# Two slices of the first feed-forward block placed among the first attention, its out products in the bank of its scores, head pairs in turns in the score product

## The chip, the cores and the metric

The kernel runs on one core of a Trainium2 chip. A core has a matrix engine (TensorE, "PE" in the profile; its weight loads are listed apart as "PEld"), a vector engine (VectorE, "DVE"), a scalar engine (ScalarE, "ACT"), a general engine (GpSimd, "POOL") and a queue that issues the transfers (SyncE, "SP"). Each engine works through its own queue in order and they wait for each other by semaphores. The metric is the device time of one execution in microseconds (us); the time of a kernel is the median of several runs.

## The reference: what is computed

Causal attention with a memory term, then two gated feed-forward blocks, on 4 sequences of 576 tokens with 8 heads of 64 (a model width of 512), all in float32:

```python
scores = scale * q @ k^T            # masked causally, softmax over the keys
local  = softmax(scores) @ v
q_p    = where(q > 0, q, exp(q) - 1) + 1
mem    = (q_p @ M_prev) / (q_p @ z_prev + 1e-06)
x      = g * mem + (1 - g) * local  # g = sigmoid(beta), one per head
x      = x / sqrt(mean(x * x) + 1e-06) * rms_g
x      = (silu(x @ w_gate) * (x @ w_val)) @ w_out          # 512 -> 1536 -> 512
x      = (sigmoid(x @ w_gate2) * (x @ w_val2)) @ w_out2    # 512 -> 1536 -> 512
```

The weights arrive as float64 (`in_w8`), are read as 16-bit pieces and put together as float32 on the core.

## The kernel before

**Groups of tokens.** The work is cut into five groups `g`. Group -1 holds the first 128 tokens of all four sequences (512 columns), groups 0 to 3 hold the other 448 tokens of one sequence each. For every group the attention comes first and then the two feed-forward blocks `l = 0, 1`, each in 12 slices `f` of 128 hidden units (`NF`). `hidden` computes one slice: gate product `pg` and value product `pv` (`mm3`, 12 matmuls each, L511), tanh on ScalarE (L526) and two products on VectorE (L528, L529). `out_share` multiplies the slice with its part of `w_out` into four PSUM banks `po0` to `po3` (L545 for group -1, L548 for the others).

**The attention of the next group rides along.** While group `g` is in its feed-forward blocks, the attention of group `g + 1` is issued in 34 steps (`att_steps`), some after each `out_share`: `att_v` (loads v into `x`), then for each head `att_qk` (loads `kd`, `qd`; L164 to L169), `att_scores` (L182 to L302), `att_av`, and for each pair of heads `att_mem`, at the end `att_norm` and four `att_xT`. Only group -1 has nothing to ride on: its attention, `att_first`, stands at the head of the kernel.

**The first attention.** For each sequence b, `att_scores0` runs once for the even heads (j = 0) and once for the odd (j = 1): one matmul writes the mask over a whole bank `po{(2b+j) % 4}` (L210), four matmuls of 64 rows add the scores of four heads (L219), VectorE takes the maxima (L221, L222), ScalarE the exponentials (L226), TensorE transposes the four blocks in place (L231), ScalarE copies them to SBUF (L235). `att_mem` makes the memory term: `e = exp(q)` on ScalarE (L347), `min(e, 1)` and `max(q, 0)` on GpSimd (L349, L350), and two matmuls per pair of heads, one for `e` and one for `q` (L369); `mem_out` (L335 to L339) writes `x`. For the sequence before, `att_av0` makes the out products (L244) in a bank of the pool `psm` (two banks, tag `mm`, the same that `pg` and `pv` use), VectorE scales them (L316 to L320) and GpSimd adds them to `x` (L248). `att_norm` squares `x` on ScalarE (L391) and takes the root on GpSimd (L396), `att_xT` scales `x` into `xn` (L401), transposes it on TensorE (L406) and splits the result into a high part (ScalarE, L410) and a low part (VectorE, L411): that is `xt`, the input of the feed-forward.

**Weights.** `weights(g, l, f)` returns gate, value and output weights of a slice (m = 0, 1, 2). In group -1 each is loaded raw (512 KB, `load_raw`, L456), put together on ScalarE and VectorE (L462, L465), written back to DRAM for the later groups (`kept`, 256 KB, L496), and gate and value are split into two parts (L425, L426). The raw pieces use 4 buffers of the pool `wp` and 2 of the later pool `wl`; the split weights use a ring of `NEARLY = 3` buffers in `wp` and `NLATE = 4` in `wl`.

**Memory.** The tiles of the first attention lie in a pool `zp` that is closed when `att_first` has been traced. The pools `hp` (output weights `wo`, the slice tiles `t` and `h`) and `wl` are opened behind it and take the same memory, so each of their tiles waits until the tiles of `zp` under it have had their last use.

**Order.** A planner at build time gives each engine its queue: it takes the instructions in the order of the program as they become ready on its own estimate of the times, so a later instruction that is ready can stand ahead of an earlier one that isn't. `issue_after(i)` keeps the instructions of a block behind `i` in the queue of `i`'s engine. In the kernel before the weights and steps that are traced up to slice 3 stand behind the last maxima and exponentials of the first attention (L624, L625); from then on there is no such bound. The last part reads, in short:

```python
xt = att_first()
zctx.close()
early_ws = [weights(-1, 0, f) for f in range(2)]     # slices 0 and 1
for o, m in ((0, 256), (256, 256)):                  # first the columns of sequences 0 and 1
    for f in range(early):
        hidden(ws[f], l, f, m, g, xt, hs[f], o)
```

## Time and profile before

| what | us |
|---|---|
| runs, median (lowest to highest of 3) | 1108.96 (1106.51 to 1110.95) |
| the profiled execution, its own time | 1107.19 |
| the profiled execution, its span (first to last instruction) | 1105.4 |
| TensorE busy in the span | 1084.5 |
| VectorE busy | 684.2 |
| ScalarE busy | 484.5 |
| GpSimd busy | 86.1 |

The profile is of one execution. Its span is 1.8 us shorter than the time of the same execution, and that time is 1.8 us below the median of the runs. Busy times of the engines overlap. The mean granted TensorE clock over the span was 0.987 of full speed (full is 2.4 GHz, the lower level 1.2 GHz).

### The profile page before, as it was taken

Reading aid. Unit: us, or ns where it says so; the run is one execution under the profiler, and the core shown is the slowest. Engines: PE = TensorE matmul, PEld = TensorE weight load, DVE = VectorE, ACT = ScalarE, POOL = GpSimd, SP = SyncE. Lnnn points to the kernel's source line nnn. Section 1 sums busy time; section 2 is a strip of 40 time slices with the busy share of each in tenths; the row PEclk is TensorE's granted clock in tenths of the full one; section 3 lists DMA queues with packets and bytes.
Section 4 is the critical chain, followed back from the end, with each engine's and each line's share of the span. In section 5 each row is a group of like instructions: output and inputs, shape, how many; then the busy total and the mean of one; then the engine's idle time right before and its main releaser. Section 6 shows DMA issues by size and latency. Waiting matters only on the chain.

```text
span 1105.4 us, 17395 instructions
## 1 busy us (share of the span) xinstructions
PE 1084.5 (98%) x6420; PEld 940.3 (85%) x6420; DVE 684.2 (62%) x1373; ACT 484.5 (44%) x905; POOL 86.1 (8%) x70
## 2 busy tenths in 40 slices
PE   8889999999999999999999999999999999999997
PEld 6766676767779999999999899999989999999997
DVE  5796869766678899866666855656785542222111
ACT  6575557655456556544344533333354322112111
POOL 4300000100000010100100100000101000000000
PEclk8889999999999999999999999999999999999999
DMA  9398878876899988978866666786655557776650
GB/s 329 108 317 297 260 243 258 249 252 204 300 333 339 357 282 307 314 240 268 249 210 209 215 211 208 251 262 207 222 190 192 198 185 245 217 218 216 213 168 34
DMA packets 93844, 264.61 MB, mean 239 GB/s; under 512 B 11072, under 2 KB 17216, under 8 KB 93632
## 3 DMA queue, kind: packets, MB, share of 16 engines
q1 hardware_dynamic: 93760, 263.50, 72.3%
q8 instruction: 51, 0.84, 0.3%
q14 instruction: 33, 0.27, 0.1%
HBM read 202.12 MB, written 61.34 MB: 238 GB/s over the span
## 4 chain that ended last, share of the span: by engine, by line
PE 92%; DMA 3%; DVE 2%; ACT 1%; issue 1%; POOL 0%; SPq 0%; ACTq 0%; DVEq 0%
PE pg L511 27%; PE pv L511 27%; PE po L548 21%; PE po L545 7%; PE ps L182 4%; PE pm L369 1%; PE pav L308 1%; PE pav L310 1%; DMA raw<-in_w 1%; PE pav L309 1%; PE pxt L406 1%; DMA rawl<-in_w 1%; DMA ph<-in_qT 1%; DMA qk<-in_qk 0%; DMA kd<-in_kT 0%
## 5 line engine op out<-in xcount | busy, mean ns | idle before, releaser
L526 ACT ACTIVATE t<-pg 128x448 f32<-128x448 f32 (+2 forms) x122 | 66.4, 544 | 185.1 <-PE pg L511 184.9
L533 ACT CAST h<-t 128x448 fp32r<-128x448 f32 x96 | 54.2, 564 | 126.4 <-DVE t L531 68.7
L292 POOL PARTITION_ALL_REDUCE mb<-mx x32 | 57.2, 1789 | 629.0 <-DVE mx L288 532.1
L531 DVE SCALAR_TENSOR_TENSOR t<-t,pv 128x448 f32<-128x448 f32 (+1 forms) x60 | 37.8, 630 | 94.4 <-PE pv L511 90.5
L545 PE MATMUL po<-t,wo 128*128 128x512 f32 x192 | 86.6, 594 | 0.0
L534 DVE TENSOR_TENSOR h<-t,h 128x448 fp32r<-128x448 f32 x96 | 60.4, 629 | 33.2 <-ACT h L533 32.6
L548 PE MATMUL po<-h,wr 128*128 128x448 f32 x360 | 79.6, 365 | 0.0
L548 PE MATMUL po<-h,wl 128*128 128x448 f32 x348 | 77.3, 368 | 0.2 <-ACT h L533 0.2
L528 DVE SCALAR_TENSOR_TENSOR t<-t,pg 128x448 f32<-128x448 f32 (+2 forms) x62 | 38.1, 615 | 59.4 <-ACT t L526 59.0
L548 PEld LDWEIGHTS po<-h,wr 128*128 128x128 f32 x360 | 66.7, 188 | 4.5
L173 ACT ACTIVATE sc<-sc 128x1536 f32<-128x1536 f32 x32 | 47.6, 1488 | 51.6 <-DVE sc L301 42.5
L548 PEld LDWEIGHTS po<-h,wl 128*128 128x128 f32 x348 | 64.9, 188 | 6.0 <-ACT h L533 0.5
L264 ACT COPY sc<-ps 128x448 f32<-128x448 f32 (+3 forms) x128 | 47.4, 374 | 51.5 <-DVE sc L259 33.0
L545 PEld LDWEIGHTS po<-t,wo 128*128 128x128 f32 x192 | 36.4, 191 | 36.4 <-issue 34.4
L511 PE MATMUL pv<-xt,wl 128*128 128x448 f32 (+2 forms) x276 | 63.4, 374 | 3.0 <-DVE t L529 2.9
L511 PE MATMUL pg<-x,wl 128*128 128x448 f32 (+1 forms) x252 | 61.7, 384 | 0.3 <-ACT t L526 0.3
L511 PE MATMUL pv<-x,wl 128*128 128x448 f32 (+1 forms) x264 | 62.0, 377 | 0.0
L176 DVE TENSOR_TENSOR pt<-sc,pt 128x1536 f16<-128x1536 f32 x32 | 56.1, 1754 | 7.6 <-ACT pt L175 7.6
L511 PEld LDWEIGHTS pv<-xt,wl 128*128 128x128 f32 x276 | 51.0, 196 | 8.3 <-DVE t L529 3.1
L511 PE MATMUL pg<-xt,wl 128*128 128x448 f32 (+1 forms) x252 | 57.7, 375 | 0.0
L548 PE MATMUL po<-h,ws 128*128 128x448 f32 x264 | 57.0, 363 | 0.0
L182 PE MATMUL ps<-qq,kk 128*128 128x448 f32 (+2 forms) x160 | 55.0, 348 | 1.9 <-ACT sc L257 1.2
(154 smaller groups left out, 2448.0 us busy)
## 6 DMA issues: line engine op xcount, KB each, us to landing
wl<-parts SPq DMA_DIRECT2D x68, 512.0 KB, 3.7
wr<-parts SPq DMA_DIRECT2D x68, 512.0 KB, 4.0
ws<-parts SPq DMA_DIRECT2D x48, 512.0 KB, 3.9
raw<-in_w SPq DMA_DIRECT2D x48, 511.8 KB, 5.3
w<-kept SPq DMA_DIRECT2D x72, 256.0 KB, 4.9
wrl<-parts SPq DMA_DIRECT2D x32, 512.0 KB, 3.5
kept<-w SPq DMA_DIRECT2D x48, 256.0 KB, 3.9
rawl<-in_w SPq DMA_DIRECT2D x24, 511.8 KB, 5.3
```

The source lines that it names most:

```text
L173: nc.scalar.activation(out=sc[:, 0:n], in_=sc[:, 0:n], func=AF.Exp, scale=scale)
L176: nc.vector.tensor_tensor(out=pt[:, 1, 0:n], in0=sc[:, 0:n], in1=pt[:, 0, 0:n], op=ALU.subtract)
L182: nc.tensor.matmul(ps[:, c0:c0 + n], kk[:, k0:k0 + 128], r[:, q0:q0 + n], start=(i == 0), stop=(i == 1 and not mask))
L264: nc.scalar.copy(out=sc[:, d:d + n], in_=ps[:, c:c + n])
L292: nc.gpsimd.partition_all_reduce(mb[:, 0:448], mx[:, 0:448], channels=128, reduce_op=bass_isa.ReduceOp.max)
L511: nc.tensor.matmul(ps[:, 0:n], w[:, a, k * 128:(k + 1) * 128], x[:, b, k, o:o + n], start=(i == 0), stop=(i == 3 * KD - 1))
L526: nc.scalar.activation(out=t, in_=pg[:, 0:n], func=AF.Tanh, scale=0.5)
L528: nc.vector.scalar_tensor_tensor(out=t, in0=t, scalar=1.0, in1=pg[:, 0:n], op0=ALU.add, op1=ALU.mult)
L533: nc.scalar.copy(out=hh[:, 0, 0:n], in_=t)
L534: nc.vector.tensor_tensor(out=hh[:, 1, 0:n], in0=t, in1=hh[:, 0, 0:n].bitcast(F32), op=ALU.subtract)
L545: nc.tensor.matmul(po[d][:, 0:n], w[2][:, c], t[:, 0:n], start=(f == 0), stop=(f == NF - 1))
L548: nc.tensor.matmul(po[d][:, 0:n], w[2][:, a, c], hh[:, b, 0:n], start=(f == 0 and i == 0), stop=(f == NF - 1 and i == 2))
```

## The change

- Slices 0 and 1 are begun inside `att_first`: their gate and value weights are requested before the first scores, and the first half of each slice (the 256 columns of sequences 0 and 1) is traced behind the transposed input of sequence 1 (slice 0) and of sequence 2 (slice 1). The second halves (`hidden(..., 256)`) stay behind the first attention. For this the ring of split weights is 4 buffers in `wp` and 3 in `wl`, and the tile `t` moves to `wp`, so neither depends on `zp`. The output weights (m = 2) of the two slices are requested after the first attention, as before, and the pool `wl` is opened ahead of `hp`.
- The out products of the first attention go to the bank that held the scores of the same sequence and head parity, so `psm` is left to `pg` and `pv`.
- In the score product the two head parities take turns: q and k of the even heads are in rows 0 to 63, of the odd heads in rows 64 to 127, and the matmuls alternate between them, into two banks.
- In the memory term `max(q, 0)` moves from GpSimd to VectorE as one instruction that also adds it to `e`; there is one matmul per pair of heads where there were two. `e` has two buffers for four sequences, so `exp(q)` of sequences 2 and 3 waits until the square of sequence 0 or 1 has used `e` as its scratch. The scaled scores and `xn` use fewer or other buffers (`xn` takes the place of q).
- The copy of the transposed weights of the odd heads goes from ScalarE to VectorE.
- All steps of group 0's attention that are traced in group -1 stand behind the last instructions of the first attention on ScalarE and VectorE (L410 and L411 for sequence 3).

```diff
--- before.py
+++ after.py
@@ -26,8 +26,8 @@
 SO = (0, 448, 896, 1216, 1408)
 SW = 1536
-NEARLY = 3
-NLATE = 4
+NEARLY = 4
+NLATE = 3
 NRAW = 4
@@ -190,54 +190,60 @@
     def att_load0():
         for b in range(B):
-            z["e", b] = zp.tile([128, NMAX], F32, tag=f"ze{b}", name="e0")
+            z["e", b] = zp.tile([128, NMAX], F32, tag=f"ze{b % 2}", name="e0")
             qk = zp.tile([128, 2, NMAX], F32, tag=f"zqk{b}", name="qk0")
             z["q", b], z["k", b] = qk[:, 0], qk[:, 1]
             nc.sync.dma_start(out=qk, in_=qk0[b])
-            for j in range(2):
-                z["s", b, j] = zp.tile([128, NMAX], F32, tag=f"zs{b}{j}", name="s0")
             if b == 1:
                 z["v"] = zp.tile([128, B, NMAX], F32, tag="zv", name="v0")
                 nc.sync.dma_start(out=z["v"], in_=v[:, 0:128, :].rearrange("b s d -> s b d"))
             if b < 2:
                 first_raw.append(load_raw(0, 0, b))
-    def att_scores0(b, j):
-        q, k, sc = z["q", b], z["k", b], z["s", b, j]
-        r = slice(64 * j, 64 * j + 64)
-        ps = pso.tile([128, NMAX], F32, tag=f"po{(2 * b + j) % 4}", name="ps0")
-        nc.tensor.matmul(
-            ps.rearrange("p (a k) -> p a k", a=NP),
-            tri_b,
-            ident_b[:, None, :].to_broadcast([128, NP, 128]),
-            start=True,
-            stop=False,
-        )
+    def att_scores0(b):
+        q, k = z["q", b], z["k", b]
+        pss = [pso.tile([128, NMAX], F32, tag=f"po{(2 * b + j) % 4}", name="ps0") for j in range(2)]
+        for ps in pss:
+            nc.tensor.matmul(
+                ps.rearrange("p (a k) -> p a k", a=NP),
+                tri_b,
+                ident_b[:, None, :].to_broadcast([128, NP, 128]),
+                start=True,
+                stop=False,
+            )
         for p in range(NP):
             c = slice(128 * p, 128 * p + 128)
-            nc.tensor.matmul(ps[:, c], q[r, c], k[r, c], start=False, stop=(p == NP - 1))
-        m = ap_.tile([128, NP], F32, tag="m0", bufs=2, name="m0")
-        nc.vector.tensor_reduce(out=m, in_=ps.rearrange("p (a k) -> p a k", a=NP), op=ALU.max, axis=AX.X)
-        z["dve", b, j] = nc.vector.tensor_scalar(out=m, in0=m, scalar1=-scale, scalar2=None, op0=ALU.mult)
-        rs = ap_.tile([128, NP], F32, tag="rs", bufs=4, name="rs")
-        for p in range(NP):
-            c = slice(128 * p, 128 * p + 128)
-            z["act", b, j] = nc.scalar.activation(
-                out=sc[:, c], in_=ps[:, c], func=AF.Exp, scale=scale, bias=m[:, p:p + 1], accum_out=rs[:, p:p + 1]
-            )
-        for p in range(NP):
-            c = slice(128 * p, 128 * p + 128)
-            nc.tensor.transpose(ps[:, c], sc[:, c], ident)
-        if j == 0:
-            z["p"] = zp.tile([128, 2, 512], F32, tag="zp", name="pt0")
-        pt = z["p"][:, j]
-        nc.scalar.copy(out=pt, in_=ps)
-        st["pt", -1, b, j] = pt, rs
+            for j in range(2):
+                r = slice(64 * j, 64 * j + 64)
+                nc.tensor.matmul(pss[j][:, c], q[r, c], k[r, c], start=False, stop=(p == NP - 1))
+        z["p"] = zp.tile([128, 2, 512], F32, tag="zp", name="pt0")
+        for j, ps in enumerate(pss):
+            m = ap_.tile([128, NP], F32, tag="m0", bufs=2, name="m0")
+            nc.vector.tensor_reduce(out=m, in_=ps.rearrange("p (a k) -> p a k", a=NP), op=ALU.max, axis=AX.X)
+            nc.vector.tensor_scalar(out=m, in0=m, scalar1=-scale, scalar2=None, op0=ALU.mult)
+            rs = ap_.tile([128, NP], F32, tag="rs", bufs=4, name="rs")
+            sc = zp.tile([128, NMAX], F32, tag=f"zs{j}", bufs=2, name="s0")
+            for p in range(NP):
+                c = slice(128 * p, 128 * p + 128)
+                nc.scalar.activation(
+                    out=sc[:, c], in_=ps[:, c], func=AF.Exp, scale=scale, bias=m[:, p:p + 1], accum_out=rs[:, p:p + 1]
+                )
+            for p in range(NP):
+                c = slice(128 * p, 128 * p + 128)
+                nc.tensor.transpose(ps[:, c], sc[:, c], ident)
+            pt = z["p"][:, j]
+            if j == 0:
+                nc.scalar.copy(out=pt, in_=ps)
+            else:
+                nc.vector.tensor_copy(pt, ps)
+            st["pt", -1, b, j] = pt, rs, ps
     def att_av0(b, j):
-        pt, rs = st.pop(("pt", -1, b, j))
-        ps = psm.tile([128, NP, 65], F32, tag="mm", name="pav0")
+        pt, rs, ps = st.pop(("pt", -1, b, j))
+        ps = ps[:, 0:NP * 65].rearrange("p (a d) -> p a d", d=65)
         for p in range(NP):
             h = 2 * p + j
             c = slice(128 * p, 128 * p + 128)
@@ -345,10 +351,9 @@
         if g < 0:
             q, e = z["q", u], z["e", u]
             nc.scalar.activation(out=e, in_=q, func=AF.Exp)
             nc.gpsimd.tensor_scalar(out=e, in0=e, scalar1=1.0, scalar2=None, op0=ALU.min)
-            nc.gpsimd.tensor_scalar(out=q, in0=q, scalar1=0.0, scalar2=None, op0=ALU.max)
-            phi = (e, q)
+            nc.vector.scalar_tensor_tensor(out=e, in0=q, scalar=0.0, in1=e, op0=ALU.max, op1=ALU.add)
+            phi = (e,)
         else:
             ph = ap_.tile([128, 512], F32, tag="ph", bufs=1, name="ph")
             e = ap_.tile([128, 512], F32, tag="xn", bufs=2, name="phe")
@@ -387,7 +392,7 @@
         x = st[g]["x"]
         ss = ap_.tile([128, 4], F32, tag="ss", bufs=2, name="ss")
         for t in range(t0, t1):
-            junk = z["s", t, 0] if g < 0 else ap_.tile([128, DM], F32, tag="xn", bufs=2, name="junk")
+            junk = z["e", t] if g < 0 else ap_.tile([128, DM], F32, tag="xn", bufs=2, name="junk")
             nc.scalar.activation(out=junk, in_=x[:, t, :], func=AF.Square, accum_out=ss[:, t:t + 1])
         s_ = ss[:, t0:t1]
         nc.vector.tensor_scalar(out=s_, in0=s_, scalar1=1.0 / DM, scalar2=1e-6, op0=ALU.mult, op1=ALU.add)
@@ -397,7 +402,7 @@
     def att_xT(g, t, xt):
         s = st[g]
-        xn = z["s", t, 1] if g < 0 else ap_.tile([128, DM], F32, tag="xn", bufs=2, name="xn")
+        xn = z["q", t] if g < 0 else ap_.tile([128, DM], F32, tag="xn", bufs=2, name="xn")
         nc.vector.scalar_tensor_tensor(
             out=xn, in0=s["x"][:, t, :], scalar=s["ri"][:, t:t + 1], in1=g_bc, op0=ALU.mult, op1=ALU.mult
         )
@@ -407,13 +412,15 @@
         o = 64 if g >= 0 and t == 3 else 0
         c0 = 128 * t
         n = 128 - o
-        nc.scalar.copy(out=xt[:, 0, :, c0:c0 + n], in_=ps[:, :, o:128])
-        nc.vector.tensor_tensor(
+        hi = nc.scalar.copy(out=xt[:, 0, :, c0:c0 + n], in_=ps[:, :, o:128])
+        lo = nc.vector.tensor_tensor(
             out=xt[:, 1, :, c0:c0 + n],
             in0=ps[:, :, o:128],
             in1=xt[:, 0, :, c0:c0 + n].bitcast(F32),
             op=ALU.subtract,
         )
+        if g < 0:
+            z["last"] = hi, lo
     late, first_raw = {}, []
@@ -473,11 +480,11 @@
     kept, parts = {}, {}
-    def weights(g, l, f):
+    def weights(g, l, f, blocks=(0, 1, 2)):
         out = []
-        for m in range(3):
+        for m in blocks:
             key = (l, f, m)
             if key in parts:
                 w = slot(g)
@@ -534,7 +541,7 @@
             nc.vector.tensor_tensor(out=hh[:, 1, 0:n], in0=t, in1=hh[:, 0, 0:n].bitcast(F32), op=ALU.subtract)
     def htiles(g):
-        t = late["h"].tile([128, NMAX], F32, tag="t", bufs=3, name="t")
+        t = wp.tile([128, NMAX], F32, tag="t", bufs=3, name="t")
         return t, (late["h"].tile([128, 2, NMAX], F32R, tag="h", bufs=3, name="h") if g >= 0 else None)
     def out_share(w, h, po, f, n):
@@ -594,48 +601,47 @@
             yield lambda t=t: next_xT(g, t)
     def att_first():
         att_load0()
         load_consts()
         st[-1] = dict(x=ap_.tile([128, 5, DM], F32, tag="x", name="x"))
         xt = xtile("xt")
+        ws = [weights(-1, 0, f, (0, 1)) for f in range(2)]
+        hs = [htiles(-1) for f in range(2)]
         for b in range(B + 1):
             if b < B:
-                for j in range(2):
-                    att_scores0(b, j)
+                att_scores0(b)
                 att_mem(-1, b)
             if b > 0:
                 for j in range(2):
                     att_av0(b - 1, j)
                 att_norm(-1, b - 1, b)
                 att_xT(-1, b - 1, xt)
-        return xt
+            if b in (2, 3):
+                hidden(ws[b - 2], 0, b - 2, 256, -1, xt, hs[b - 2], 0)
+        return xt, ws, hs
     def next_xT(g, t):
         if t == 0:
             st["xt"] = xtile("xt")
         att_xT(g, t, st["xt"])
-    xt = att_first()
+    xt, early_ws, early_hs = att_first()
     zctx.close()
+    late["w"] = ctx.enter_context(tc.tile_pool(name="wl", bufs=1, reuse_waits="tile"))
     late["h"] = ctx.enter_context(tc.tile_pool(name="hp", bufs=1, reuse_waits="tile"))
-    late["w"] = ctx.enter_context(tc.tile_pool(name="wl", bufs=1, reuse_waits="tile"))
-    early_ws = [weights(-1, 0, f) for f in range(2)]
-    gated = ExitStack()
-    gated.enter_context(tc.issue_after(z["dve", 3, 1].ins))
-    gated.enter_context(tc.issue_after(z["act", 3, 1].ins))
+    for f in range(2):
+        early_ws[f] += weights(-1, 0, f, (2,))
     for g in range(-1, B):
         n = 512 if g < 0 else S - 128
         steps = list(att_steps(g + 1)) if g + 1 < B else []
         total = 2 * NF - 4
         done, used = 0, 0
         for l in range(2):
             early = 2 if g < 0 and l == 0 else 0
-            ws = early_ws[:early]
-            hs = [htiles(g) for f in range(early)]
-            for o, m in ((0, 256), (256, 256)):
-                for f in range(early):
-                    hidden(ws[f], l, f, m, g, xt, hs[f], o)
+            ws, hs = early_ws[:early], early_hs[:early]
+            for f in range(early):
+                hidden(ws[f], l, f, 256, g, xt, hs[f], 256)
             po = None
             for f in range(NF + 1):
                 if f < NF:
@@ -643,16 +649,19 @@
                         ws.append(weights(g, l, f))
                         hs.append(htiles(g))
                         hidden(ws[f], l, f, n, g, xt, hs[f])
-                    if g < 0 and l == 0 and f == 3:
-                        gated.close()
                 if f > 0:
                     if po is None:
                         po = [pso.tile([128, NMAX], F32, tag=f"po{d}", name="po") for d in range(KD)]
                     out_share(ws[f - 1], hs[f - 1], po, f - 1, n)
                     done += 1
-                    while used < len(steps) and used < len(steps) * done // total:
-                        steps[used]()
-                        used += 1
+                    with ExitStack() as after:
+                        if g < 0:
+                            for i in z["last"]:
+                                after.enter_context(tc.issue_after(i.ins))
+                        while used < len(steps) and used < len(steps) * done // total:
+                            steps[used]()
+                            used += 1
             xn = xtile("x1") if l == 0 else None
             for d in range(KD):
                 evacuate(l, d, n, g, po[d], xn)
```

## Rows read from the trace of the kernel before

**Rows 1.** The page, part 1: busy us (share of the span) xinstructions

```profile
PE 1084.5 (98%) x6420; PEld 940.3 (85%) x6420; DVE 684.2 (62%) x1373; ACT 484.5 (44%) x905; POOL 86.1 (8%) x70
```

**Rows 2.** Stretches: length; busy PE, PEld, DVE, ACT, POOL; clock, DMA share, GB/s

```profile
30.00:40.00 10.00, 9.04 (x74) 8.12 (x73) 8.73 (x29) 8.42 (x34) 4.20 (x5) 1.00 0.01 3
20.00:52.71 32.71, 27.68 (x207) 24.80 (x206) 22.49 (x69) 19.01 (x60) 12.19 (x14) 0.92 0.46 145
52.71:72.99 20.28, 15.97 (x86) 13.96 (x87) 16.92 (x34) 15.18 (x37) 2.37 (x2) 0.75 0.93 327
120.00:317.00 197.00, 197.00 (x1035) 138.63 (x1034) 144.76 (x269) 112.74 (x203) 11.72 (x8) 1.00 0.78 256
```

**Rows 3.** Chain that ended last, 0:66 us: start, length, what

```profile
20.07 6.86 DMA ph<-in_qT
...
51.19 7.13 DMA rawl<-in_w
...
62.24 0.50 PE pv L511 x2
```

**Rows 4.** Timeline of ScalarE: start, length, instruction, [idle before <-releaser]

```profile
26.95 0.58 ACT L356 ACTIVATE phe<-ph 128x448 f32<-128x448 f32 x1 [1.07 <-DMA ph<-in_qT]
27.44 0.61 ACT L391 ACTIVATE s<-x 128x512 f32<-128x512 f32 x1
...
42.78 0.69 ACT L164 ACTIVATE kk<-kd 128x576 fp32r<-128x576 f32 x1 [2.41 <-DMA kd<-in_kT]
43.38 0.61 ACT L391 ACTIVATE s<-x 128x512 f32<-128x512 f32 x1
```

**Rows 5.** Timeline of TensorE, 0:82 us, same columns

```profile
6.46 2.82 PE L219 MATMUL ps<-qk 64*128 64x128 f32 x32
...
29.72 1.16 PE L219 MATMUL ps<-qk 64*128 64x128 f32 x8
...
60.65 0.47 PE L182 MATMUL ps<-qq,kk 128*128 128x448 f32 x1 [1.25 <-ACT sc L257]
...
61.91 0.23 PE L186 MATMUL ps<-tri_b,ident_b 128*128 128x128 bf16 x1
...
67.03 1.60 PE L511 MATMUL pv<-xt,ws 128*128 128x256 f32 x12
68.47 1.60 PE L511 MATMUL pg<-xt,ws 128*128 128x256 f32 x12
72.99 2.93 PE L511 MATMUL pv<-xt,wl 128*128 128x256 f32 x12 [2.92 <-DVE t L529]
```

**Rows 6.** Waits of the issuing queue, 0:120 us: total, times, longest

```profile
SPq L158 <- DVE r L338: 14.1, 1, 14.1
```

**Rows 7.** Groups of VectorE, 20:52.71 us: busy us, mean ns, idle before

```profile
L401 DVE SCALAR_TENSOR_TENSOR s<-x,ri,g_bc 128x512 f32<-128x512 f32 x4 | 3.0, 745 | 1.4 <-POOL ri L396 1.4
...
L166 DVE TENSOR_TENSOR kk<-kd,kk 64x576 fp32r<-64x576 f32 x2 | 1.5, 756 | 1.1 <-ACT kk L164 1.1
...
L169 DVE TENSOR_TENSOR q<-qd,qq 64x448 fp32r<-64x448 f32 x2 | 1.2, 586 | 0.0
...
L465 DVE SCALAR_TENSOR_TENSOR w<-raw,top 128x512 int32<-128x512 int32 x1 | 0.7, 693 | 1.4 <-ACT top L462 1.4
...
L358 DVE SCALAR_TENSOR_TENSOR ph<-ph,phe 128x448 f32<-128x448 f32 x1 | 0.6, 626 | 0.0
```

**Rows 8.** Timeline of VectorE, 0:76 us

```profile
9.09 0.17 DVE L222 TENSOR_SCALAR m<-m 128x4 f32<-128x4 f32 x1
...
9.89 0.53 DVE L222 TENSOR_SCALAR m<-m 128x4 f32<-128x4 f32 x1
...
52.02 0.69 DVE L411 TENSOR_TENSOR xt<-pxt,xt 128x512 fp32r<-128x512 f32 x1 [1.28 <-ACT xt L410]
...
72.52 0.41 DVE L529 TENSOR_TENSOR t<-t,pv 128x256 f32<-128x256 f32 x1
```

**Rows 9.** Timeline of GpSimd, 0:75 us

```profile
9.78 2.95 POOL L350 TENSOR_SCALAR qk<-qk 128x512 f32<-128x512 f32 x2
```


## The prediction

> **What bounds the kernel now.** I read the page's busy shares first, then the busy time by stretches, then the chain that ended last, then the queues one by one. TensorE is busy 1084.5 of 1105.4 us [rows 1], and from 120 to 317 us its busy time is the whole stretch at full clock [rows 2]: there only fewer matmuls would help, and this change takes none away. So the gain can lie only in the head, where TensorE waits. The reader is to see two parts there. Up to 52.71 us (end of L411 at 52.02 [rows 8]) the first attention runs: from 20 us on TensorE is busy 27.68 of 32.71 us and VectorE 22.49, with no engine full [rows 2]. From 52.71 to 72.99 the feed-forward starts badly: 16.0 us busy in 20.28 at a mean clock of 0.75, while the DMA engines are busy 0.93 [rows 2].
>
> Two things in the head are not the first attention's own. The chain runs through the transfer `ph<-in_qT` (20.07 to 26.93) [rows 3], which belongs to group 0: ScalarE's instruction for it stands ahead of the square of sequence 0 and idles 1.07 us; later `kk` of group 0 idles 2.41 us on its transfer, ahead of the square of sequence 2 [rows 4]. And the chain then waits 7.13 us for a raw weight in the late pool, until pv of slice 1 starts at 62.24 [rows 3]. The DMA engines had been empty before (0.01 busy from 30 to 40 us [rows 2]): the issuing queue stood 14.1 us at a load of group 0's keys (L158) [rows 6], and the late pool's buffers lay under the first attention's.
>
> **The change, part by part.** I call T the time at which the last transposed input (L411 of sequence 3) is done: 52.71 before. From T on TensorE has everything but its feeding, so the span is T, plus the matmuls left, plus the stalls after T.
>
> *Matmuls left after T.* Before, at 72.99, one half-slice product of slices 0 and 1 is left (the pv that starts there) and 1105.4 - 72.99 = 1032.4 us follow. After, at T, the four second-half products are left, three more. One costs 68.47 - 67.03 = 1.44 us [rows 5]: 4.3 us. Before, group 0's scores of two heads are done by then; behind the new bound on ScalarE and VectorE they are not. From 60.65 to 62.14 (61.91 + 0.23) three of a head's five blocks run, 960 of 1600 columns, in 1.49 us [rows 5]; a head is 2.5 us, two are 5.0. So the span is T + 1032.4 + 4.3 + 5.0 = T + 1041.7, plus stalls. The four first-half products, 5.8 us, lie before T. TensorE has 32.71 - 27.68 = 5.0 us idle there before the change [rows 2], and gains room by the memory term's halved matmuls and by the foreign waits that go, so I cost them at nothing; without that cover they cost 5.8.
>
> *When T comes.* VectorE gets more work, so I count it from 20 us, where the first inputs are in. Before it is 22.49 us busy up to 52.71 [rows 2]. Group 0's share goes behind T: L166 1.5, L169 1.2, L358 0.6 [rows 7], leaving 19.2. Added are: `max(q, 0) + e` for sequences 2 and 3, twice 0.745 by the nearest row, L401, of the same kind and size [rows 7], 1.5 (those of sequences 0 and 1 fall before 20 us); three copies of transposed weights, by L411, equally 128x512 out of PSUM, 0.69 each [rows 8], 2.1; the second value weight, which came after T before, twice 0.69 by L465 [rows 7], 1.4; the first halves' products, four of 0.41 [rows 8], 1.6. Together 25.8 us. How densely VectorE works is not in the trace of before; it is bounded from below by that stretch's own 22.49 / 32.71 = 0.69, and from above by 1. I take the densest stretch of the first attention, 8.73 in 10 us [rows 2], because the two waits that thinned it out (1.07 and 2.41 us on ScalarE) go behind T: 25.8 / 0.873 = 29.5, T = 49.5. The ends are 45.8 and 57.4.
>
> *Stalls after T.* Before, from 52.71 to 72.99, TensorE did five half-slice products (7.2 us) and most of two heads (4.6): 11.8 us in 20.28, a stall of 8.5. Its largest part, slice 1's value weights in the late pool, goes: all four split weights now lie in `wp`. What stays is that VectorE takes its queue in order: the product L529 at 72.52 frees the bank for which TensorE had waited 2.92 us [rows 5, 8]. The half-clock start there (2.93 us for a product that takes 1.6 at full clock [rows 5]) may recur. The two together are 4 us, which I take; the ends are 0 and 8.5. The queues that the requests of slices 0 and 1 are moved past: the issuing queue gets them ahead of group 0's loads, four raw loads that fit its empty time, and GpSimd loses L350, 2.95 us for two [rows 9].
>
> *Edits off this path.* Waiting of the scores of sequences 2 and 3 for the bank of the out products of 0 and 1: bounded by 0 and by one out product with its scaling; VectorE's sum holds that work already, so 0. The alternating score products: the trace has 32 records in 2.82 us (0.088 each) at 6.46 and 8 in 1.16 (0.145) at 29.72 [rows 5]. If alternation gives the first pace to sequences 2 and 3, 32 records save 1.8 us of TensorE, which isn't what sets T: 0, at most 1.8 of gain; a loss of the same size is the other end. The Trainium skill, page "TensorEngine Tiling (Array Packing)", section "Theoretical Speedup", allows up to 2 times for contractions of 64 rows; by it the records would come to 0.073 and the saving to 2.8 us, off the path too.
>
> One thing speaks against the move from GpSimd to VectorE: beside L350 (from 9.78 [rows 9]) a small VectorE instruction takes 0.53 us that takes 0.17 just before [rows 8]. I take 0.36 us for each of two, inside the rounding of T. The Trainium skill, page "SBUF — State Buffer", section "Who interferes with whom", says that a VectorE instruction with two SBUF inputs contends with GpSimd's reads; by that each of the two could lose a whole GpSimd instruction, which by L350 is 1.5 us, and the time would come out 3 us later, within the forecast's own spread.
>
> **Sum.** 49.5 + 1041.7 + 4 = 1095.2 of span, and with the 1.8 us around it a time of 1097.0, against 1107.2 of the profiled execution. The runs of before lie 0.7 below to 3.8 above that execution, so I leave 1097 as it is and let the range take up the scatter.
>
> **Rivals.**
> *B, everything fits.* VectorE is nearly never idle from 20 us and no stall follows: 45.8 + 1041.7 + 1.8 = 1089. For it: the DMA engines were empty for long, so weights can lie ready at T. Against: VectorE's chain still passes through ScalarE, GpSimd and TensorE for every sequence.
> *C, the feeding stays late.* The loads of the output weights and of slice 2 still wait in the issuing queue behind a load of group 0, whose release is now bound to T, or the planner puts the first halves behind T; then the stall of 8.5 stays, with T = 49.5: 1101.5; if part of the first halves slips too, up to 1107. For it: the 14.1 us stand at L158 [rows 6]. Against: slices 0 and 1 no longer depend on the late pool.
> *D, slower.* One mechanism, in `att_mem` of sequences 2 and 3: with two buffers for `e` their chain begins only behind the square of sequences 0 and 1. That chain already is the longest: 27.44 to 43.38 from square 0 to square 2 [rows 4]. In series come exp (0.6), GpSimd's minimum (1.5) and the new VectorE instruction (0.75), 2.9 us, and before the transposes two half-slice products in TensorE's queue, 2.9: T = 52.7 + 5.8 = 58.5; with the stall of 8.5 kept, 58.5 + 1041.7 + 8.5 + 1.8 = 1110.5. It decides from T + stall = 63.7 on. Against it: the square of sequence 0 itself stood behind the foreign wait and comes earlier now.
>
> **How the numbers follow.** Forecast 0.55, B 0.17, C 0.18, D 0.10. The forecast's own spread is 1092 to 1102. The range, 1087 to 1107, takes in B, C and the bounds of T and stall but for their worst sum, and leaves D out. A measurement of this kernel can tell about 0.5% from no change, 5.5 us: faster is below 1103.4. Faster: the forecast nearly whole, B, and half of C, 0.79. Same: the rest of C and some of D, 0.14. Slower: 0.07.
>
> **What would show it.** Right: L411 of sequence 3 ends between 46 and 53 us; pg and pv of slice 0 with 256 columns stand before it; no ScalarE or VectorE instruction of group 0 stands before it; TensorE without gaps at full clock from some 4 us behind it on. Wrong: VectorE idle for over 30% from 20 us to T, then T is late and the chain names `exp(q)` of sequence 2 or the banks of the scores; or the chain behind T names a raw weight again, then C holds; or TensorE's groups from 120 us on are slower, which nothing here foresees.

## The result, and the profile after

| what | before | after |
|---|---|---|
| median of the runs (lowest to highest of 4) | 1108.2 (1106.51 to 1110.95) | 1098.18 (1096.88 to 1099.43) |
| profiled execution, time and span | 1107.19, 1105.4 | 1096.88, 1095.1 |
| T, the end of the last transposed input | 52.71 | 51.59 |
| span behind T | 1052.7 | 1043.5 |

The ratio of after to before is 0.991, with a 95% interval of 0.9887 to 0.9933: 10 us. The forecast was 1097.0. In these two profiled executions T itself moved by only 1.1 us; the other 9 us lie behind T. The body of the kernel is as long as it was: from the first output product of group 0 to the end 783.9 us remained before and 783.6 remain after.

The busy time of the engines, from the page of after (against [rows 1]; us, share of the span, instructions):

```profile
PE 1076.3 (98%) x6388; PEld 932.8 (85%) x6388; DVE 684.7 (63%) x1381; ACT 482.7 (44%) x901; POOL 78.8 (7%) x66
```

TensorE lost 8.2 us of busy time: half of the memory term's matmuls are gone, and less of its work runs at half clock. The stretches of the head of after (against [rows 2]; stretch, its length, then busy time and instructions of PE, PEld, DVE, ACT and POOL, the granted clock, the DMA engines' share and GB/s):

```profile
20.00:51.59 31.59, 27.87 (x205) 24.41 (x203) 23.98 (x74) 17.35 (x57) 11.24 (x14) 0.93 0.42 130
30.00:40.00 10.00, 9.47 (x77) 8.42 (x75) 9.47 (x32) 8.62 (x37) 6.00 (x8) 1.00 0.19 75
40.00:50.00 10.00, 7.85 (x68) 7.64 (x66) 6.75 (x18) 2.81 (x7) 3.06 (x5) 1.00 0.01 2
51.59:57.00 5.41, 5.41 (x25) 5.31 (x25) 3.70 (x7) 1.18 (x3) 0.00 (x0) 0.50 1.00 385
57.00:90.00 33.00, 31.50 (x136) 21.43 (x134) 32.39 (x57) 28.32 (x55) 4.20 (x3) 1.00 0.99 331
```

Up to T, VectorE is busy 23.98 of 31.59 us, 0.76. It is nearly full from 30 to 40 us, and 6.75 of 10 from 40 to 50, where the chain of the last two sequences and the products of the first halves are left. Behind T, TensorE runs at half clock until 57, then VectorE is full: 32.39 of 33 us. TensorE's timeline of after (start, duration, engine, line, operation, shapes, count, and in brackets the idle time before with its releaser):

```profile
7.08 2.06 PE L220 MATMUL ps<-qk 64*128 64x128 f32 x32
...
29.34 1.16 PE L220 MATMUL ps<-qk 64*128 64x128 f32 x8
...
41.78 1.48 PE L518 MATMUL pv<-xt,ws 128*128 128x256 f32 x11
43.10 1.06 PE L374 MATMUL pm<-mzt,e 128*128 128x130 f32 x8
43.91 1.68 PE L518 MATMUL pg<-xt,ws 128*128 128x256 f32 x12
45.43 1.60 PE L518 MATMUL pv<-xt,ws 128*128 128x256 f32 x12
46.87 0.60 PE L411 MATMUL pxt<-ident,qk 128*128 128x128 f32 x4
49.62 0.63 PE L411 MATMUL pxt<-ident,qk 128*128 128x128 f32 x4 [2.15 <-DVE qk L406]
...
51.65 2.71 PE L518 MATMUL pg<-xt,ws 128*128 128x256 f32 x11
...
76.91 0.36 PE L182 MATMUL ps<-qq,kk 128*128 128x192 f32 x1 [0.96 <-ACT sc L270]
...
80.93 3.06 PE L518 MATMUL pv<-xt,ws 128*128 128x512 f32 x12 [0.55 <-DVE t L536]
```

The four first-half products run from 40.15 to 47.0, ahead of the transposes of the last two sequences (46.87 and 49.62). They do stand before work of the first attention: the memory product of sequence 3 (43.10) comes behind slice 0's two, the transposes of sequence 2 (46.87) behind all four. The chain that ended last leads through slice 0's two on its way to T:

```profile
41.94 1.32 PE pv L518 x11
43.26 0.91 PE pm L374 x8
```

Two of the four are not new, though. Before had slice 0's two ahead of T already, so the change brings forward slice 1's two, 2.9 us:

```profile
43.05 1.68 PE L511 MATMUL pg<-xt,ws 128*128 128x256 f32 x12
44.57 1.60 PE L511 MATMUL pv<-xt,ws 128*128 128x256 f32 x12
```

Behind T the four second halves follow, with scores of group 0 between them, without a gap.

The queues of ScalarE and VectorE at T:

```profile
50.28 0.59 ACT L415 CAST xt<-pxt 128x512 fp32r<-128x512 f32 x1 [2.19 <-PE pxt L411]
50.77 0.69 ACT L164 ACTIVATE kk<-kd 128x576 fp32r<-128x576 f32 x1
...
50.90 0.69 DVE L416 TENSOR_TENSOR xt<-pxt,xt 128x512 fp32r<-128x512 f32 x1 [1.43 <-ACT xt L415]
51.62 0.76 DVE L166 TENSOR_TENSOR kk<-kd,kk 64x576 fp32r<-64x576 f32 x1
```

T is 50.90 + 0.69. In the queues of both engines group 0's instructions (L164, L166) stand behind the splits of sequence 3 (L415, L416); the waits of [rows 4] are gone. The issuing queue of after:

```profile
26.93 0.38 SPq L463 DMA_DIRECT2D raw<-in_w  x1
49.53 0.38 SPq L124 DMA_DIRECT2D x<-in_v  x1
...
50.55 1.17 SPq L463 DMA_DIRECT2D rawl<-in_w  x2
```

It stands for 22 us, longer than the 14.1 us of [rows 6], now at group 0's v (L124), and the output weights of slices 0 and 1 are requested only at 50.55. TensorE did not wait for them; ScalarE did, 2.47 us, before it took up the first at 57.26.

### The profile page after: what moved, and what is told of

Its sections match the earlier page's. It is cut to its first block, busy times and chain, and to the rows that moved or that the text cites. A ratio compares the mean times of both kernels' runs of the same rounds, so it can differ in the third digit from the quotient of the medians.

```text
span 1095.1 us, 17324 instructions
## 1 busy us (share of the span) xinstructions
PE 1076.3 (98%) x6388; PEld 932.8 (85%) x6388; DVE 684.7 (63%) x1381; ACT 482.7 (44%) x901; POOL 78.8 (7%) x66
## 4 chain that ended last, share of the span: by engine, by line
PE 91%; DMA 4%; DVE 2%; ACT 1%; issue 0%; SPq 0%; POOL 0%; DVEq 0%; ACTq 0%
PE pv L518 27%; PE pg L518 27%; PE po L555 21%; PE po L552 7%; PE ps L182 4%; PE pm L374 1%; PE pav L314 1%; PE pav L316 1%; PE pav L315 1%; DMA raw<-in_w 1%; DMA qk<-in_qk 1%; PE pxt L411 1%; DMA kd<-in_kT 1%; DMA rawl<-in_w 1%; DMA qd<-in_qT 1%
## 5 line engine op out<-in xcount | busy, mean ns | idle before, releaser
L555 PE MATMUL po<-h,ws 128*128 128x448 f32 x348 | 75.8, 364 | 0.0
L555 PEld LDWEIGHTS po<-h,ws 128*128 128x128 f32 x348 | 64.9, 188 | 4.5
L518 PE MATMUL pg<-x,ws 128*128 128x448 f32 (+1 forms) x264 | 64.1, 383 | 0.8 <-ACT x L561 0.6
L518 PE MATMUL pv<-xt,ws 128*128 128x448 f32 (+2 forms) x288 | 63.5, 365 | 0.5 <-DVE t L536 0.5
L518 PE MATMUL pv<-x,ws 128*128 128x448 f32 (+1 forms) x264 | 62.4, 375 | 0.0
L518 PE MATMUL pg<-xt,ws 128*128 128x448 f32 (+2 forms) x276 | 60.3, 367 | 0.7 <-ACT xt L415 0.7
L555 PE MATMUL po<-h,wl 128*128 128x448 f32 x264 | 58.6, 367 | 0.2 <-ACT h L540 0.2
L518 PEld LDWEIGHTS pv<-xt,ws 128*128 128x128 f32 x288 | 51.9, 194 | 5.9 <-DVE t L536 1.0
L518 PEld LDWEIGHTS pg<-x,ws 128*128 128x128 f32 x264 | 48.9, 188 | 9.0 <-issue 1.9
```

What stands on the lines that cost most here:

```text
L518: nc.tensor.matmul(ps[:, 0:n], w[:, a, k * 128:(k + 1) * 128], x[:, b, k, o:o + n], start=(i == 0), stop=(i == 3 * KD - 1))
L555: nc.tensor.matmul(po[d][:, 0:n], w[2][:, a, c], hh[:, b, 0:n], start=(f == 0 and i == 0), stop=(f == NF - 1 and i == 2))
```

## The experiments

For each kernel T is given, and the **stall**: span - T - 1041.7, by the prediction's formula, less another 5.8 where the first halves stand behind T. For after it is 1095.1 - 51.59 - 1041.7 = 1.8 us. For before, with slice 1's two first-half products (2.9 us) behind T, it is 1105.4 - 52.71 - 1041.7 - 2.9 = 8.1 us.

| kernel | median us | ratio to before, 95% | span | T | stall |
|---|---|---|---|---|---|
| after | 1098.18 | 0.9887 to 0.9933 | 1095.1 | 51.59 | 1.8 |
| `b_weights` | 1099.38 | 0.9905 to 0.9933 | 1101.8 | 54.52 | 5.6 |
| `u_halves` | 1097.9 | 0.9898 to 0.9925 | 1096.2 | 50.77 | 3.7 |
| `u_gate` | 1099.63 | 0.991 to 0.9936 | 1096.6 | 53.38 | 1.5 |
| `u_phi` | 1101.89 | 0.9938 to 0.9964 | 1102.1 | 55.31 | 5.1 |
| `h_behind` | 1106.53 | 0.9974 to 1.0002 | 1104.2 | 50.11 | 6.6 |
| `bw_behind` | 1109.95 | 1.0 to 1.002 | 1109.6 | 54.14 | 8.0 |
| `u_e4` | 1100.74 | 0.9907 to 0.9958 | 1096.8 | 49.01 | 6.1 |
| `v_head` | 1101.77 | 0.9916 to 0.9961 | 1102.3 | 57.09 | 3.5 |
| `v_tfirst` | 1095.04 | 0.9855 to 0.9895 | 1097.6 | 56.33 | -0.4 |
| `v_tfirst_e4` | 1092.98 | 0.9835 to 0.9878 | 1092.1 | 50.10 | 0.3 |
| `h_tfirst` | 1099.1 | 0.9893 to 0.9928 | 1097.1 | 49.67 | -0.1 |
| `u_avturns` | 1102.41 | 0.9922 to 0.9963 | 1102.3 | 58.62 | 2.0 |

T, the stall and the span are of one profiled execution, the median of 4 to 12 runs. How far T scatters is shown with `v_tfirst`.

**One part alone: the weights early (`b_weights`).** The kernel before, with the gate and value weights of slices 0 and 1 requested ahead of the first scores; the scratch tiles are shared to make room.

```diff
-NEARLY = 3
-NLATE = 4
+NEARLY = 4
+NLATE = 3
...
-        t = late["h"].tile([128, NMAX], F32, tag="t", bufs=3, name="t")
+        t = wp.tile([128, NMAX], F32, tag="t", bufs=3, name="t")
...
+        ws = [weights(-1, 0, f, (0, 1)) for f in range(2)]
...
-    early_ws = [weights(-1, 0, f) for f in range(2)]
+    for f in range(2):
+        early_ws[f] += weights(-1, 0, f, (2,))
```

> The kernel before with one part of the change alone: gate and value weights of slices 0 and 1 are requested ahead of the first attention into four buffers of wp, and the tile t lies in wp (the first attention's scratch tiles share buffers to make room). First halves, gate of the steps, memory term, banks and score order stay as before. T is the end of the split of sequence 3's transposed input. Theory (the gain lies behind T, in slices 0 and 1 no longer waiting for the late pool): T stays near 52.7 us, the stretch behind it loses most of its 8.5 us of stall, time 1101 to 1103. Rival (the gain comes from the attention itself, by the gate and the memory term): the time stays within 3 us of before, 1105 to 1110.

Measured 1099.38, 1.2 us from after and below the theory's 1101 to 1103. This edit alone brings nearly all of the gain. But the trace shows more than the edit says: with the weights there, the planner itself put all four first-half products ahead of T (44.70 to 52.1), where before had two. So this run does not tell the two apart, and the next ones were made for that.

**The first halves traced behind the first attention (`u_halves`).**

```diff
-            if b in (2, 3):
-                hidden(ws[b - 2], 0, b - 2, 256, -1, xt, hs[b - 2], 0)
...
-            for f in range(early):
-                hidden(ws[f], l, f, 256, g, xt, hs[f], 256)
+            for o in (0, 256):
+                for f in range(early):
+                    hidden(ws[f], l, f, 256, g, xt, hs[f], o)
```

> The changed kernel, but the first halves of slices 0 and 1 stand behind the first attention, as the second halves do. Theory (the four products cost part of what they bring, because they stand in TensorE's queue ahead of the memory term and the transposes of sequences 2 and 3): T falls from 51.6 to about 49, 5.8 us of products come behind it, time 1101 to 1102. Rival 1 (they lie in idle time of TensorE at no cost): T stays at 51.6, time 1104. Rival 2 (they cost as much as they bring): T falls to 46, time 1098.

Measured 1097.9. The number is rival 2's, but not for its reason: T is 50.77 and not 46. The planner put the products ahead of T again (39.4 to 46.7), so the place in the program decides nothing and this run says nothing on what they cost.

**The first halves bound behind T (`h_behind`).** The same edit, and the second stretch is kept behind the last transpose of the first attention in TensorE's queue.

```diff
+            with ExitStack() as behind:
+                if early:
+                    behind.enter_context(tc.issue_after(z["pe"].ins))
                 for o in (0, 256):
```

> The changed kernel, with the first halves of slices 0 and 1 bound behind the last transpose of the first attention in TensorE's queue. In u_halves the planner had put them ahead of T all the same (from 39.4 us, T 50.8), because their weights and the tile t were there; so that run could not tell what they cost. Theory (they cost part of what they bring): T falls to 48 to 49.5, 5.8 us of products come behind it, time 1100 to 1102. Rival 1 (no cost): T stays at 51.6, time 1104. Rival 2 (cost as large as the gain): T falls to 46, time 1098.

Measured 1106.53: the gain is gone, 8.4 us more than after. The theory and both rivals missed. 5.8 us are the products; T came 1.5 us earlier in the profile, 50.11, so at least 2.6 us are something else. TensorE's timeline of this kernel shows it:

```profile
76.10 5.49 PE L518 MATMUL pg<-xt,wl 128*128 128x512 f32 x12 [4.69 <-DVE t L535]
```

An idle time of 4.69 us, and then 12 matmuls in 5.49 us that take 3.06 at full clock. VectorE's queue ahead of that `t`:

```profile
69.72 1.09 DVE L299 TENSOR_TENSOR sc<-sc,mb 128x896 f32<-128x896 f32 x1 [1.53 <-POOL mb L298]
70.72 0.74 DVE L146 SCALAR_TENSOR_TENSOR vl<-x,sv,vh 128x512 f16<-128x512 f32 x1
71.39 0.95 DVE L307 TENSOR_TENSOR sc<-sc,mb 128x320 f32<-128x320 f32 x3
72.26 0.62 DVE L291 TENSOR_TENSOR mx<-sc 128x448 f32<-128x448 f32 x1
...
75.02 0.69 DVE L472 SCALAR_TENSOR_TENSOR w<-rawl,top 128x512 int32<-128x512 int32 x1
75.63 0.42 DVE L535 SCALAR_TENSOR_TENSOR t<-t,pg 128x256 f32<-128x256 f32 x1
```

The `t` that frees TensorE's bank stands behind the softmax of group 0 (L299, L307, L291), and that had waited for GpSimd's maximum. No product of the first slices needs the result of that softmax. Before shows the same picture: the `t` at 72.52, for which TensorE had idled 2.92 us [rows 5, 8], stands behind the same instructions of group 0 (L293 at 68.91, L301 at 69.91, L285 at 70.78).

**The same bound on `b_weights` (`bw_behind`).**

```diff
+            with ExitStack() as behind:
+                if early:
+                    behind.enter_context(tc.issue_after(z["pe"].ins))
                 for o in (0, 256):
```

> The kernel of b_weights (before, with weights and t of slices 0 and 1 in wp; 1099.4 us, the planner had put all four first-half products ahead of T there too), with the first halves bound behind the last transpose of the first attention. It parts the two gains of those buffers: products that can be done in the first attention's idle time, and slices 0 and 1 fed at once behind T. Theory (the larger part is the feeding): 1101 to 1104. Rival (the larger part is the products done ahead of T): 1105 to 1108.

Measured 1109.95, no gain at all (1.0 to 1.002). With the weights in place and the first halves behind T, TensorE idles 3.94 us for a `t` (79.25), and a half-clock gate product of 5.49 us follows at 79.73. The stall is 8.0 us, as long as before's 8.1: the theory that the late pool's weights were the stall fell. It does not follow that early weights are worth nothing in time: this kernel has all four first-half products behind T and before only two, which is 2.9 us more work there, while the median rose by 1.4 us and the profile's T by 1.4. What the weights gave back, if anything, was not measured by itself.

**The order on VectorE (`h_tfirst`, `v_tfirst`).** `h_behind` and after, each with group 0's steps bound behind the newest slice's tanh (ScalarE) and `t` product (VectorE), where they were bound behind the last transposed input alone.

```diff
-        nc.scalar.activation(out=t, in_=pg[:, 0:n], func=AF.Tanh, scale=0.5)
+        ta = nc.scalar.activation(out=t, in_=pg[:, 0:n], func=AF.Tanh, scale=0.5)
...
-            nc.vector.tensor_tensor(out=t, in0=t, in1=pv[:, 0:n], op=ALU.mult)
+            td = nc.vector.tensor_tensor(out=t, in0=t, in1=pv[:, 0:n], op=ALU.mult)
...
+        z["t"] = ta, td
...
-                            for i in z["last"]:
+                            for i in z["t"]:
```

> All four first halves behind the last transpose of the first attention, as in the earlier experiment that gave 1106.5 us with an idle time of 4.69 us before t at 76.10, now with t bound ahead of group 0's steps on VectorE and ScalarE. Theory: of the 8.4 us that the place of the first halves was worth, 5.8 us are their own TensorE time and the rest is VectorE's order; with the order mended the time is 1102 us (1101 to 1103.5). Rival: it is VectorE's load, and the time stays at 1105.5 to 1107 us.

Measured 1099.1: 7.4 us less than `h_behind`, by the order alone, and better than the theory. The edit binds on ScalarE and VectorE together; the two were not tried singly. TensorE's only idle time between T and 90 us, and what VectorE does ahead of that `t`:

```profile
56.80 2.93 PE L518 MATMUL pg<-xt,ws 128*128 128x256 f32 x12 [1.94 <-DVE t L535]
...
55.72 0.69 DVE L472 SCALAR_TENSOR_TENSOR wo<-rawl,top 128x512 int32<-128x512 int32 x1 [3.28 <-ACT top L469]
```

The `t` (56.33) stands behind an output weight whose raw piece came late: with the order mended, the loads of rival C are the next wait. So with the first halves behind T nearly the whole gain is there if `t` does not queue behind group 0.

> The changed kernel, with the steps of group 0 that are traced ahead bound behind the latest slice's tanh on ScalarE and the latest t product on VectorE (before: behind the last transposed input alone). Theory: behind T, TensorE waits for t, which stands in VectorE's in-order queue behind group 0's attention; with t ahead of it the idle times of 0.96 us (76.91) and 0.55 us (80.93) go, T stays near 51.6, and the time is 1095 to 1097 us. Rival: what matters there is the sum of VectorE's work, 32.39 of 33.0 us from 57 to 90, and not its order; then the time stays at 1098 us. A third way: group 0's attention itself comes too late for the third and fourth slice, and the time is 1100 us or more.

Measured 1095.04, as the theory said; against after 3.1 us, with intervals that overlap a little. Its stall is -0.4. The profiled execution is its slowest run (1099.41) and teaches how far to trust one T. Up to T its queues hold the same instructions in the same order as after, yet T is 56.33 and not 51.59. The second raw weight reached ScalarE at 26.09 instead of 24.22, and then (stretches of `v_tfirst`, columns as above):

```profile
30.00:31.00 1.00, 0.09 (x1) 0.00 (x0) 1.00 (x6) 0.52 (x1) 0.45 (x1) 1.00 0.86 336
31.00:33.00 2.00, 2.00 (x9) 1.78 (x8) 1.77 (x8) 2.00 (x13) 0.59 (x1) 0.54 0.98 384
33.00:35.00 2.00, 2.00 (x9) 1.34 (x8) 1.61 (x5) 1.52 (x7) 1.74 (x3) 0.50 0.16 63
35.00:37.00 2.00, 2.00 (x10) 1.77 (x10) 0.90 (x4) 0.08 (x1) 1.13 (x1) 0.50 0.00 0
```

TensorE did almost nothing for one microsecond, then the granted clock was at the lower level until past 37. In after, the idle time at the same place (29.04) is 0.36 us and the clock stays at 1.00. A T that differs by 4 or 5 us between two single profiles proves nothing; the medians do.

**Four buffers of `e` (`u_e4`, `v_tfirst_e4`).**

```diff
-            z["e", b] = zp.tile([128, NMAX], F32, tag=f"ze{b % 2}", name="e0")
+            z["e", b] = zp.tile([128, NMAX], F32, tag=f"ze{b}", name="e0")
```

> The changed kernel with four buffers for e, so that exp(q), minimum and sum of sequences 2 and 3 no longer wait for the squares of sequences 0 and 1. Theory (the chain by the squares is one of the things that set T): T falls by 1 to 3 us, time 1095.5 to 1097.5. Rival (TensorE's queue and the squares themselves set T): T within 0.7 us of 51.6, time 1098.

T came at 49.01, 2.6 us earlier in these single profiles, as expected, but the time was 1100.74, not the theory's 1095.5 to 1097.5; its seven runs lie between 1096.89 and 1106.93, and it can't be told from after. TensorE's timeline of `u_e4`:

```profile
75.55 5.34 PE L518 MATMUL pg<-xt,wl 128*128 128x512 f32 x12 [3.56 <-DVE t L535]
```

It is the wait of `h_behind` once more: `t` at 74.81 stands behind L299, L307 and L291 of group 0. The earlier T was given back there.

> The same order (t ahead of group 0's attention) together with a buffer of e for each of the four sequences. With four buffers alone T came 2.6 us earlier, 49.01, and the gain was lost behind T to an idle time of 3.56 us before t and a weak clock after it. Theory: the loss was one of order, so here T is near 49.0 and the time 1093.5 to 1096 us. Rival: the loss is VectorE's load (38.04 of 40.99 us from T to 90), and the time is 1098 to 1101 us, whatever the order.

Measured 1092.98, the fastest of all (0.9835 to 0.9878, clear of after's interval). T 50.10, and the same place in its timeline, with the longest idle time ahead of it:

```profile
57.48 7.36 PE L553 MATMUL po<-t,wo 128*128 128x512 f32 x16 [1.56 <-DVE wo L472]
...
71.07 3.07 PE L518 MATMUL pg<-xt,wl 128*128 128x512 f32 x12 [0.63 <-DVE t L535]
```

0.63 us in place of 3.56, and full clock. The loss was one of order: no work is removed, but the edit also moves some of VectorE's out of this stretch (from T to 90 us it is busy 32.06 of 39.90 us in place of 38.04 of 40.99). Here too the wait that is left is for an output weight.

**The raw weights later (`v_head`).** `u_e4`, and the two raw loads that were requested among the loads of sequences 0 and 1 come behind them.

```diff
-            if b < 2:
-                first_raw.append(load_raw(0, 0, b))
```

> The changed kernel with four buffers for e, and with the two raw loads of slice 0 requested behind those of q, k, v, the memory matrices and the norm's weights, where they stood between them. Theory (the first attention starts late because of the order of the first transfers: in the changed kernel the chain goes through 9.2 and 11.7 us of transfers up to 24.2 us): the first product with the memory matrices starts 2 to 3 us earlier, T falls by 3 to 5 us, time 1093.5 to 1096. Rival (VectorE's load from 20 us on sets T, as the prediction had it): T falls no more than in u_e4.

Measured 1101.77: missed by 5.8 us and more. The first memory product started at 15.22 instead of 20.25, as meant, but ScalarE then stood 2.22 us before 35.40 and TensorE was at half clock from 30 until past 38; T was 57.09. The half clock came behind an idle time of 1.92 us before 28.92, in which TensorE waited for VectorE's scaling (L404). An earlier start of sequence 0 alone did not bring T forward; whether it would without that idle time was not tested.

**The gate on group 0 (`u_gate`).** Its steps behind the last maxima and exponentials again.

```diff
-                            for i in z["last"]:
+                            for i in (z["act"], z["dve"]):
```

> The changed kernel, but the steps of group 0's attention stand behind the last maxima and exponentials of the first attention and not behind its last transposed input. Theory (the two foreign waits, 1.07 and 2.41 us, come back ahead of the squares, but group 0's scores come earlier as well): T rises by 2 to 4 us, work behind T falls by up to 5, time 1097 to 1101. Rival (the bound is worth the whole gain): 1105 or more.

Measured 1099.63, inside the theory's span, 1.45 us above after with overlapping intervals: of this part only the sign of the median is seen.

**The memory term (`u_phi`).**

```diff
-            nc.vector.scalar_tensor_tensor(out=e, in0=q, scalar=0.0, in1=e, op0=ALU.max, op1=ALU.add)
-            phi = (e,)
+            nc.gpsimd.tensor_scalar(out=q, in0=q, scalar1=0.0, scalar2=None, op0=ALU.max)
+            phi = (e, q)
```

> The changed kernel with the memory term of before: max(q, 0) on GpSimd, two matmuls for each pair of heads. Theory (TensorE gets 16 matmuls back, some 3.5 us, GpSimd four instructions of 1.5 us, VectorE loses four of 0.7; the chain of sequences 2 and 3 runs through TensorE and GpSimd): T rises by 1 to 3 us, time 1099 to 1101. Rival (VectorE's load sets T, so its relief brings T forward): T falls by 1 to 3 us, time 1095 to 1097.

Measured 1101.89, 3.7 us above after with separate intervals: right in sign, larger than the theory.

**Bank and turns undone together (`u_avturns`).**

```diff
-        for p in range(NP):
-            c = slice(128 * p, 128 * p + 128)
-            for j in range(2):
-                r = slice(64 * j, 64 * j + 64)
+        for j in range(2):
+            r = slice(64 * j, 64 * j + 64)
+            for p in range(NP):
+                c = slice(128 * p, 128 * p + 128)
...
-        ps = ps[:, 0:NP * 65].rearrange("p (a d) -> p a d", d=65)
+        ps = psm.tile([128, NP, 65], F32, tag="mm", name="pav0")
```

> The changed kernel with two small parts undone together: the out products of the first attention take their bank from the pool of the other matmuls again, and the score product does the four heads of one half, then the four of the other. Theory: both are off the path that sets the end, 1097 to 1099.7 us, within 1.5 us of the changed kernel, and T within 1.5 us of 51.59. Rival: the alternation's pace (32 records in 2.06 against 2.82 us, for each of four sequences) or the banks let the chain go on sooner, and without them the time is 1101 us or more.

Measured 1102.41, 4.2 us above after (the intervals overlap by 0.0011): the theory that both parts are off the path most likely fell. The timelines of TensorE and ScalarE of `u_avturns`:

```profile
44.47 1.48 PE L518 MATMUL pv<-xt,ws 128*128 128x256 f32 x11
...
46.23 1.89 PE L250 MATMUL pav<-v,pt 128*128 128x64 f32 x16
...
49.66 0.38 ACT L533 ACTIVATE t<-pg 128x256 f32<-128x256 f32 x1 [0.90 <-PE pg L518]
50.04 0.63 ACT L396 ACTIVATE e<-x 128x512 f32<-128x512 f32 x1
```

The out products share two banks with `pg` and `pv` again. Those of sequence 2 (46.23) run behind slice 0's first half, and its square (L396) stands at 50.04, behind slice 1's tanh, where it is at 40.55 in after. The turns are seen in the 32 records at 7 us, which are those of sequences 0 and 1 together: 2.06 us with them, 2.82 (at 7.09) without. The stall is 2.0 us, like after's, so what this profile lost lies ahead of T (58.62). The trace points to the bank, but this is argued: the two parts were not run singly.

## Why the prediction was right, and where it was not

**When T comes** was too early by 2.1 us: 51.59 against 49.5, within the 46 to 53 that were named. VectorE's work was 23.98 us against 25.8, 1.8 us too much; 1.1 of it are two instructions of [rows 2]'s stretch that go behind T as well and that I left in (L357, 0.40 us at 27.56, and an output weight's L465, 0.69 at 50.05). Its density was the mis-sized term, 0.76 against 0.873. By itself it would have put T 4.5 us later than forecast (25.8 / 0.76); the smaller work took 2.4 of them back. The stretch of 30 to 40 us is even denser than I took (9.47), but from 20 to 30 the raw weights arrive (ScalarE and VectorE wait 2.64 and 1.99 us for one) and from 40 the chain of two sequences leaves VectorE at 6.75 of 10. The densest stretch of a phase is no measure for its two ends.

**Stalls after T** were 1.8 us against 4 by the formula. The two errors nearly cancel (+2.1 and -2.2), which is why 1095.2 of span met 1095.1: that is luck. Counted in the rows, what TensorE lost is nearer to the 4: 1.5 us idle from 57 to 90 us, and some 2.3 us in the two second-half products at half clock (2.71 us at 51.65 and 2.55 at 54.16 for 11 matmuls each, against 1.47 and 1.48 for the first halves). So the frame, T + 1041.7, was the term that is some 2 us too long. It took 1032.4 us from before as they were, and there the first product itself ran at half clock (2.93 us for 1.6 [rows 5]; granted clock 0.90 from 72.99 to 90). The kernels with `t` first say the same: the formula gives them a stall of -0.4, 0.3 and -0.1 us, and yet `h_tfirst` idles 1.94 us and `v_tfirst_e4` 1.56 and 0.63. Of the signs I named, full clock came 5.4 us behind T and not 4, and two idle times, 0.96 and 0.55 us, stand in what was to be without gaps.

**The reason given for the smaller stall failed.** I wrote that the largest part of the 8.5 us, slice 1's value weights in the late pool, goes because the weights lie in `wp`. `bw_behind` has them there and keeps a stall of 8.0 against before's 8.1; `h_behind` has them there too, 6.6, and with nothing but group 0's steps put behind `t` it falls to -0.1 (`h_tfirst`). The part that I named as what stays, VectorE's queue taken in order, was nearly all of it. That the same holds in before is read from its trace; before with `t` first was not run. In after it is small because two slices' first `t` products are done before group 0's steps may start, as `h_behind` shows by taking that away. So rival C's loads were the wrong suspect for this change: they are as late as it feared (50.55), and TensorE doesn't wait for them in after. They are what is left once `t` goes first (1.94 us in `h_tfirst`, 1.56 in `v_tfirst_e4`).

**The first halves at nothing.** Their cover is there: by the medians they cost 4.1 us if they stand behind T with the order mended (`h_tfirst` against `v_tfirst`) and 8.4 us without that (`h_behind` against after), against the 5.8 that I named. The cover isn't whole: 4.1 in place of 5.8 leaves 1.7 us that the products cost ahead of T, the chain of after goes through two of them, and T in the profiles is 1.5 and 1.9 us earlier without them (50.11 and 49.67). And I counted all four against the 5.0 us of idle time ahead of T, though slice 0's two were in before's busy time there already (43.05).

**Edits off this path** were not all at nothing. The memory term, which I counted as 1.5 us more for VectorE and otherwise as room, is worth 3.7 us. Bank and turns, at 0 and at most 1.8, are together worth about 4. I had looked at what the shared bank could cost (scores behind out products) and not at what the old bank costs once first halves stand in the head (out products behind `pg` and `pv`). The gate on group 0, 1.45 us, is not told from nothing. These prices hold within the changed kernel and don't add up to its gain: `b_weights` has none of these parts and is 1.2 us slower than after.

**The turns' pace** came out better than the row for sequences 0 and 1 (2.06 us for 32, 0.064 each, against 0.088). The Trainium skill, page "TensorEngine Tiling (Array Packing)", section "Theoretical Speedup", allows up to 2 times for such products; the estimate by it was 0.073, and the trace shows a little more: 2.3 times the pace of a single block (0.145), though only 1.4 times that of blocks in a row (0.088). For sequences 2 and 3, where I looked for the gain, the turns did less: sequence 3 still takes 1.16 us for each 8 records [rows 5]. Its second bank was read by VectorE until 30.27 (L326), and its scores stand behind the first bank's.

**The memory term beside GpSimd.** The new instruction takes 0.68 us at 35.15, where GpSimd has only a one-column instruction, and 1.19 at 39.87, beside GpSimd's sum at 39.10 (1.41 us): 0.51 us lost once. The Trainium skill, page "SBUF — State Buffer", section "Who interferes with whom", has the sign right; the 3 us that I worked out by it did not come.

**Rival D.** Its mechanism may exist, at a small price: four buffers of `e` gave 2.1 us in the medians of the kernels with `t` first (1095.04 to 1092.98; the intervals overlap), not the 9 us that D needed.

## What to carry to other kernels

Where an engine takes its queue in order, ask for each product on the path what a planner may put ahead of it: here binding the next group's attention behind the newest `t` was worth 3 us on the changed kernel (the intervals overlap a little) and 7.4 on the one with the first halves late, with no work removed. Two late things in one trace (a raw weight, a product) need not both be the cause; give one of them early and see whether the stall moves. And compare medians: a single profile's T differed by 4.7 us for the same order of instructions.

## What was not expected of the hardware

In `v_tfirst` one microsecond in which TensorE was busy 0.09 (30 to 31) was followed by a granted clock of 0.57 and then 0.50 until 37, where it had been 1.00; behind an idle time of 0.36 us at the same place in after it stayed at 1.00. `v_head` shows the first again: busy 0.08 from 28 to 29, and 0.50 from 30 to 38. After the idle times of 2.15 and 0.68 us before T, after's TensorE works at 0.50 until 57, though it is busy all the time. And alternating matmuls of 64 rows went at 0.064 us each where four blocks of eight, each of one parity, went at 0.088 and a single block of eight at 0.145, all at a granted clock of 1.00; why the single block is slowest was not tested.
